# A retention layer with a soft mixture of experts: the keys by tokens of step 18 made on TensorE instead of loaded

## Chip, cores, metric

One core of a Trainium2 chip. The metric is the device time of one execution in microseconds; the table below gives the median of three.

## What is computed

Two layers in a row, all in float32. The first is a decaying linear attention (retention) over B = 4 sequences, H = 8 heads, S = 768 tokens, D = 64; the second a mixture of 8 experts with 4 slots each, in which every slot reads a weighted mean of all 3,072 tokens.

```python
for t in range(S):                                   # retention
    state = gamma[None, :, None, None] * state + np.einsum('bhd,bhe->bhde', k[:, :, t], v[:, :, t])
    y[:, :, t] = scale * np.einsum('bhd,bhde->bhe', q[:, :, t], state)
x = y as (B * S, H * D)
logits = x @ phi                                     # soft mixture of experts
d = softmax of logits over the tokens;  slot_input = d.T @ x
slot_out[e] = np.maximum(slot_input[e] @ w1[e], 0.0) @ w2[e]
out = (softmax of logits over the slots) @ slot_out
```

## The kernel before

**Steps and pairs.** The retention is done in chunks of 128 tokens. A step is one chunk of one sequence; there are 24 of them, numbered chunk by chunk (step i is sequence i mod 4, chunk i // 4), and worked on in twelve pairs (`P`, steps 2P and 2P + 1). Per step: scores of keys against queries (`score_mm`, L227), a causal mask on VectorE (L235), the part of the output that comes from the state (`carry_mm`, L251), the part from within the chunk (`attend_mm`, L260), the state's update from keys and values (`state_mm`, L288), the output turned to tokens-by-features (`natural_mm`, L304, copied by ScalarE at L311), and logits and dispatch sums (L328, L384).

**Two layouts of the keys.** The scores need the keys by features (`kT`, features on the partitions), the state needs them by tokens (`kn`, tokens on the partitions). For most steps both come from memory: the input tile holds `kT`, `qT`, `v` and `kn`, 512 columns each, one load of 128 x 2048 floats (L201, 1,024 KB). Steps in the list `TURNED` (L46) load only the first three (L199, 768 KB), and `turn_k` (L203) makes `kn`: four transposes of 128 x 128 on TensorE (L206) into a PSUM bank and one copy by ScalarE (L207) into the empty quarter of the input tile. The last four steps need no `kn`, since no state follows them. The host lays the two kinds of steps out in two arrays (`x3`, `x4`, L712).

**Order.** The order on every engine is written out by hand (`manual_schedule`, L94): what the program says first, the engine does first. In the loop over pairs (L451 to L528) pair P issues the loads of steps 2P + 6 and 2P + 7 on SyncE, between weight loads (`PACE`, L45); six input tiles go round, so a load waits until the step that used the tile is done. GpSimd multiplies the new queries and values by decays (L212, L217). `turn_k` of the even step 2P + 2 stands between the state's update and `natural_mm` of pair P (L501), and uses the bank "A0", which the scores of step 2P + 2 take next.

**Behind the retention.** From about 107 us TensorE multiplies the slots by the first expert weights (L589), then by the second (L669), and combines (L650); VectorE and ScalarE copy the results (L655), and SyncE writes them out in eight transfers of 768 KB (L656). All transfers of data, in and out, are issued by SyncE and go through one queue (queue 1) over 16 DMA engines. Queues 8 and 14 carry the engines' instructions.

```python
501  if 2 * P + 2 in TURNED:
502      turn_k(2 * P + 2, "A0")
503  natural_mm(P)
504  natural_copy(P)
```

Of the kernel before, what the change touches and what calls it, by code (L numbers as in the profile page):

```python
# [42 lines left out]
NIN = 6  # L43
NRING = 9
PACE = (1, 1, 1, 2, 1, 2, 1, 2, 2, 0, 2, 2)  # L45
TURNED = (0, 1, 2, 3, 4, 8, 12, 14)  # L46
SIW = 48
LEAN = [i for i in range(1, NSTEP) if i in TURNED or i >= NSTEP - B]
FULL = [i for i in range(1, NSTEP) if i not in LEAN]
# [32 lines left out]
def retention_soft_moe_kernel(  # L82
# [120 lines left out]
    def turn_k(i, name):  # L203
        kp = bank(name)
        for g in range(NPAIR):
            nc.tensor.transpose(kp[:, g * 128:(g + 1) * 128], st[i]["kT"][:, g, :], ident)  # L206
        nc.scalar.copy(st[i]["kn"], kp.rearrange("p (h d) -> p h d", d=D))  # L207
# [83 lines left out]
    def state_add(P):  # L291
        for k in range(2):
            d = sst[(2 * P + k) % B]
            if P < B // 2:
                nc.scalar.copy(d, pr[P]["S"][:, k])
            else:
                nc.vector.tensor_tensor(d, d, pr[P]["S"][:, k], ALU.add)  # L297
# [153 lines left out]
    for P in range(NPP):  # L451
# [46 lines left out]
        if P < NPP - B // 2:  # L498
            state_mm(P)
            state_add(P)  # L500
        if 2 * P + 2 in TURNED:  # L501
            turn_k(2 * P + 2, "A0")
# [235 lines left out]
```

## Time and profile before

| | |
|---|---|
| median of 3 executions | 158.36 us (158.28 to 158.56) |
| the profiled execution, its own time | 158.41 us |
| its span, first to last instruction | 156.6 us |
| mean granted clock of TensorE | 0.984 |
| busy: TensorE / VectorE / ScalarE / GpSimd | 92% / 50% / 27% / 38% |
| DMA: moved, mean rate | 62.48 MB, 399 GB/s |
| loads of 1,024 KB / of 768 KB for steps | 12 / 11 |

The span is what the trace covers; the execution's own time has 1.8 us around it. Busy shares are means over stages that differ: up to about 103 us the retention, then the experts, and behind 149 us nothing but writes. A DMA share of 1.00 is all 16 engines busy (a share a little over that is rounding of the records). "Landing" is the moment at which a transfer's semaphore says that all of it has arrived.

### The profile page before, as it was taken

How to read it: one execution, taken by the hardware profiler on the slowest of the kernel's cores; microseconds unless marked ns; L12 is line 12 of the kernel's file. 1: busy time of each engine (PE TensorE's matmuls, PEld its weight loads, DVE VectorE, ACT ScalarE, POOL GpSimd, SP SyncE). 2: the span in 40 equal slices, each digit the busy share in tenths (PEclk: the TensorE clock that was granted, in tenths of full speed). 3: DMA queues.
4: the chain of work that ended last, by engine and by line, in shares of the span. 5: the costliest groups of instructions: out<-in, count | busy, mean ns of one | idle time of the engine just before them, and what ended most of it. 6: DMA issues, size and time to landing. Idle time of an engine off the chain costs nothing.

```text
span 156.6 us, 5484 instructions
## 1 busy us (share of the span) xinstructions
PE 144.6 (92%) x2412; PEld 107.4 (69%) x2412; DVE 77.8 (50%) x187; ACT 42.2 (27%) x100; POOL 58.8 (38%) x66
## 2 busy tenths in 40 slices
PE   7999999999999999999999979999999999999500
PEld 2688989897988789979996857864232555557200
DVE  0379337682865483768574847566010104535500
ACT  3215422333232316220613042344100001424300
POOL 1351986784936294654938283010000000000000
PEclk9999999999999999999999999999999999999985
DMA  4999999999999999999999999999999999999891
GB/s 159 421 424 421 416 419 416 416 414 419 406 423 408 423 419 410 427 398 431 404 419 412 415 411 416 400 408 421 411 428 416 423 416 416 414 415 417 348 402 78
DMA packets 9816, 62.48 MB, mean 399 GB/s; under 512 B 1088, under 2 KB 1088, under 8 KB 4544
## 3 DMA queue, kind: packets, MB, share of 16 engines
q1 hardware_dynamic: 9792, 62.13, 96.6%
q8 instruction: 19, 0.31, 0.8%
q14 instruction: 5, 0.04, 0.1%
HBM read 55.84 MB, written 6.29 MB: 397 GB/s over the span
## 4 chain that ended last, share of the span: by engine, by line
PE 92%; DVE 2%; issue 1%; DVEq 0%
PE A L227 16%; PE Y L260 15%; PE A L669 9%; PE A L304 7%; PE Y L251 6%; PE S L288 6%; PE Y L589 4%; PE A L589 4%; PE sm L328 4%; PE sm L424 3%; PE S L384 3%; PE A L206 2%; PE sm L650 2%; PE S L650 1%; PE Y L650 1%; PE Y L638 1%
## 5 line engine op out<-in xcount | busy, mean ns | idle before, releaser
L235 DVE TENSOR_TENSOR r<-A,mi 128x512 f32<-128x512 f32 (+1 forms) x50 | 30.1, 662 | 22.1 <-PE A L227 22.1
L212 POOL TENSOR_TENSOR b<-b,qtab 128x512 f32<-128x512 f32 x20 | 25.7, 1287 | 23.5 <-DMA b<-in_x_dram 18.3
L227 PE MATMUL A<-b 64*128 64x128 f32 x384 | 25.4, 280 | 0.0
L227 PEld LDWEIGHTS A<-b 64*128 64x128 f32 x384 | 22.7, 188 | 3.1 <-issue 2.0
L217 POOL TENSOR_TENSOR b<-b,kt 128x512 f32<-128x512 f32 x23 | 23.6, 1046 | 2.4 <-DMA b<-in_x_dram 2.4
L260 PE MATMUL Y<-r,b 128*64 128x128 f32 x352 | 22.5, 276 | 0.5 <-issue 0.5
L260 PEld LDWEIGHTS Y<-r,b 128*64 128x64 f32 x352 | 19.2, 137 | 2.9 <-issue 2.6
L669 PE MATMUL A<-b,r 128*32 128x128 f32 (+1 forms) x336 | 15.9, 300 | 0.0
L311 ACT COPY r<-A 128x512 f32<-128x512 f32 x23 | 12.4, 592 | 8.6 <-PE A L304 8.6
L669 PEld LDWEIGHTS A<-b,r 128*32 128x32 f32 x336 | 10.3, 109 | 6.4 <-issue 4.4
L304 PE MATMUL A<-mi,r 128*128 128x128 f32 x96 | 13.3, 278 | 0.3 <-ACT r L279 0.3
L288 PE MATMUL S<-b 128*64 128x64 f32 x304 | 11.1, 222 | 0.6 <-issue 0.6
L304 PEld LDWEIGHTS A<-mi,r 128*128 128x128 f32 x96 | 10.4, 141 | 1.7 <-ACT r L279 0.5
L288 PEld LDWEIGHTS S<-b 128*64 128x64 f32 x304 | 10.4, 138 | 0.5 <-issue 0.5
L251 PE MATMUL Y<-b,sst 64*64 64x128 f32 x304 | 10.6, 276 | 0.0
L416 POOL TENSOR_TENSOR cn<-cn,cz 128x128 f32<-128x128 f32 x6 | 2.4, 401 | 19.6 <-DVE cz L415 7.2
L280 DVE COPY r<-Y 128x512 f32<-128x512 f32 x9 | 6.2, 690 | 5.9 <-PE Y L260 5.1
L251 PEld LDWEIGHTS Y<-b,sst 64*64 64x64 f32 x304 | 8.2, 132 | 1.2
L328 PEld LDWEIGHTS sm<-r,kt 128*32 128x32 f32 x192 | 6.2, 110 | 3.3 <-issue 3.3
L408 ACT ACTIVATE cn<-cn 128x128 f32<-128x128 f32 x6 | 1.9, 310 | 21.2 <-DVE cn L407 21.2
L328 PE MATMUL sm<-r,kt 128*32 128x128 f32 x192 | 7.4, 273 | 0.0
L297 DVE TENSOR_TENSOR sst<-sst,S 128x256 f32<-128x256 f32 x16 | 6.0, 418 | 2.7 <-PE S L288 2.5
(140 smaller groups left out, 182.9 us busy)
## 6 DMA issues: line engine op xcount, KB each, us to landing
b<-in_w_dram SPq DMA_DIRECT2D x29, 1024.0 KB, 15.1
b<-in_x_dram SPq DMA_DIRECT2D x12, 1024.0 KB, 12.5
b<-in_x_dram SPq DMA_DIRECT2D x11, 768.0 KB, 10.7
out_dram<-b SPq DMA_DIRECT2D x8, 768.0 KB, 8.7
r<-in_w_dram SPq DMA_DIRECT2D x5, 512.0 KB, 11.0
b<-in_first_dram SPq DMA_DIRECT2D x1, 512.0 KB, 3.5
r<-in_first_dram SPq DMA_DIRECT2D x1, 512.0 KB, 4.3
sst<-in_w_dram SPq DMA_DIRECT2D x1, 512.0 KB, 11.7
```

Of the source, the lines that this page charges most:

```text
L212: nc.gpsimd.tensor_tensor(q, q, qtab, ALU.mult)
L217: nc.gpsimd.tensor_tensor(v, v, vsc[:, i // B, a:b].unsqueeze(2).broadcast_to([128, b - a, D]), ALU.mult)
L227: nc.tensor.matmul(s["sc"][r][:, g, :], s["kT"][half(r), g, :], s["qT"][half(r), g, :], start=True, stop=True, skip_group_check=True)
L235: nc.vector.tensor_tensor(s["A"][:, r, g:g + n], s["sc"][r][:, g:g + n], mask.unsqueeze(1).broadcast_to([128, n, C]), ALU.mult)
L251: nc.tensor.matmul(p["y"][k][b][half(half_of(r, g)), gl, :], sst[(2 * P + k) % B][half(r), g, :], s["qT"][half(r), g, :], start=(gl == 0 a ...
L260: nc.tensor.matmul(pr[P]["y"][k][g // 2][half(half_of(r, g)), g % 2, :], s["v"][:, 2 * g + r, :], s["A"][:, r, g, :], start=(P < B // 2 an ...
L288: nc.tensor.matmul(S_[half(r), k, g, :], s["kn"][:, 2 * g + r, :], s["v"][:, 2 * g + r, :], start=True, stop=True, skip_group_check=True)
L304: nc.tensor.transpose(X[k][:, g * 128:(g + 1) * 128], pr[P]["yT"][:, k, g, :], ident)
L311: (nc.scalar.copy if engines[k] == "scalar" else nc.vector.tensor_copy)(xn, pr[P]["X"][k])
L328: nc.tensor.matmul(q["ltp"][32 * j:32 * j + 32, :], phis[:, p, :], st[GRP * g + j]["yT"][:, p, :], start=(p == 0), stop=(p == NPAIR - 1), ...
L589: nc.tensor.matmul(hp[hf][32 * j:32 * j + 32, :], si0[:, a:a + NSLOT], w1t[hf, g, k][:, j * 512:(j + 1) * 512], start=(g == 0 and k == 0), ...
L669: nc.tensor.matmul(op[32 * j:32 * j + 32, :w], hT[fc // 4][:, fc % 4, 4 * g + j, :], w2t[4 * g + j, cb, fc], start=(n == 0), stop=(n == le ...
```

## The change

Step 18 joins the list. Its load is one of 768 KB from the first array, where it takes a row of its own, and pair 8 gets a `turn_k`.

```diff
-TURNED = (0, 1, 2, 3, 4, 8, 12, 14)
+TURNED = (0, 1, 2, 3, 4, 8, 12, 14, 18)
 LEAN = [i for i in range(1, NSTEP) if i in TURNED or i >= NSTEP - B]
 FULL = [i for i in range(1, NSTEP) if i not in LEAN]
```

On TensorE, in pair 8 (steps 16 and 17): the state's update (L288), the outputs' transposes (L304), and the first transpose of the probabilities (L364); A_... are PSUM tiles of the four "A" banks, S and sm those banks.

```order
 L260 MATMUL Y_1200<-r,b 64x128 x4
 L288 MATMUL S<-b 64x64 x16
-L304 MATMUL A_1255<-mi,r 128x128 x4
-L304 MATMUL A_1260<-mi,r 128x128 x4
+L206 MATMUL A_1255<-mi,b 128x128 x4
+L304 MATMUL A_1261<-mi,r 128x128 x4
+L304 MATMUL A_1266<-mi,r 128x128 x4
 L364 MATMUL sm<-mi,pT 128x128
```

Four transposes of the keys come in ahead of the outputs' transposes; everything behind keeps its order.

On ScalarE, the same pair: the copy of half of the outputs out of PSUM (L279), and the copies of the turned outputs (L311).

```order
 L279 COPY r<-Y_1199 128x2x256
-L311 COPY r<-A_1255 128x512
-L311 COPY r<-A_1260 128x512
+L207 COPY b<-A_1255 128x512
+L311 COPY r<-A_1261 128x512
+L311 COPY r<-A_1266 128x512
 L369 COPY pl<-sm 128x128
```

One copy comes in ahead of the two.

On SyncE, the loads of pair 6 (steps 18 and 19, between weight loads), and what each issue waits for (the load before on its semaphore, and the engines that used the tile).

```order
 L163 DMA b<-in_w_dram 128x2048 [waits DMAHW3_49]
-L201 DMA b<-in_x_dram 128x2048 [waits PE_49,DMAHW4_49,Activation_49,Pool_49]
+L199 DMA b<-in_x_dram 128x1536 [waits PE_49,DMAHW4_49,Activation_49,Pool_49]
 L201 DMA b<-in_x_dram 128x2048 [waits DMAHW5_49,PE_49,Pool_49]
 L163 DMA b<-in_w_dram 128x2048 [waits DMAHW6_49]
```

The load of step 18 keeps its place and its waits, and is a quarter shorter. Later in the same queue, the weight load that takes over step 18's tile waits for ScalarE too.

## Rows read from the trace of the kernel before

**Rows 1.** The page: busy us of TensorE (share, instructions) with the other engines; the DMA share in tenths and the rate in 40 slices of the span.

```profile
PE 144.6 (92%) x2412; PEld 107.4 (69%) x2412; DVE 77.8 (50%) x187; ACT 42.2 (27%) x100; POOL 58.8 (38%) x66
...
DMA  4999999999999999999999999999999999999891
GB/s 159 421 424 421 416 419 416 416 414 419 406 423 408 423 419 410 427 398 431 404 419 412 415 411 416 400 408 421 411 428 416 423 416 416 414 415 417 348 402 78
```

**Rows 2.** The chain that ended last, by engine (page); and from the table of waits: who waited for what, us in total, times, longest.

```profile
PE 92%; DVE 2%; issue 1%; DVEq 0%
...
POOL b L212 <- DMA b<-in_x_dram: 18.3, 14, 2.7
...
PEld Y L589 <- issue: 3.8, 13, 0.3
...
PEld Y L589 <- DMA b<-in_w_dram: 0.6, 2, 0.3
```

**Rows 3.** The tail by stretches: from:to and length in us; busy us of PE, PEld, DVE, ACT, POOL (instructions); granted clock, DMA share, GB/s.

```profile
138.00:146.50 8.50, 7.70 (x168) 5.33 (x167) 3.79 (x10) 2.22 (x6) 0.00 (x0) 1.00 1.02 418
146.50:149.00 2.50, 1.30 (x16) 0.45 (x12) 1.82 (x4) 1.63 (x4) 0.00 (x0) 1.00 0.69 279
149.50:152.50 3.00, 0.00 (x0) 0.00 (x0) 0.00 (x0) 0.00 (x0) 0.00 (x0) 0.82 1.02 422
152.50:153.50 1.00, 0.00 (x0) 0.00 (x0) 0.00 (x0) 0.00 (x0) 0.00 (x0) 0.50 0.61 252
153.50:155.00 1.50, 0.00 (x0) 0.00 (x0) 0.00 (x0) 0.00 (x0) 0.00 (x0) 0.50 0.19 78
```

**Rows 4.** The last four writes of the output, two by two: the issues (first and last start in us), and the us from issue to landing (least, median, most: the first and the second of each two).

```profile
L656 SPq DMA_DIRECT2D out_dram<-b x2: 332/332/332, 142.2 to 143.8; - x2
...
DMA to landing us min/median/max: 7.9/8.0/8.0
...
L656 SPq DMA_DIRECT2D out_dram<-b x2: 332/332/333, 148.3 to 149.2; - x2
...
DMA to landing us min/median/max: 5.4/5.9/6.3
```

**Rows 5.** Transfers of instructions: both queues over the whole span (count, MB, share of 16 engines' time), then queue 8 from the start to 67.0, to 71.6 and to 135.7 us; then loads in issue order, each with its time to landing: the weights issued at 50.8, step 18's input, which is next in the queue, and two neighbours among the weights issued at 113.4 and 114.4.

```profile
q8 instruction: 19, 0.31, 0.8%
q14 instruction: 5, 0.04, 0.1%
...
q8 instruction: 8, 0.13, 0.8%
...
q8 instruction: 9, 0.15, 0.8%
...
q8 instruction: 17, 0.28, 0.8%
...
L163 SPq DMA_DIRECT2D b<-in_w_dram x1: 422/422/422, 50.8 to 50.8; - x1
...
DMA to landing us min/median/max: 16.8/16.8/16.8
...
L201 SPq DMA_DIRECT2D b<-in_x_dram x1: 328/328/328, 59.6 to 59.6; - x1
...
DMA to landing us min/median/max: 12.1/12.1/12.1
...
L166 SPq DMA_DIRECT2D b<-in_w_dram x2: 327/328/328, 113.4 to 114.4; - x2
...
DMA to landing us min/median/max: 18.4/19.9/21.4
```

**Rows 6.** The pace of loads: the first four of 768 KB (steps 1 to 4), and four neighbours of 1,024 KB (two inputs, then two weight tiles); first and last issue, and us from issue to landing, of which the least is the first load's and the most the last one's.

```profile
L199 SPq DMA_DIRECT2D b<-in_x_dram x4: 424/436/442, 1.7 to 3.1; - x4
...
DMA to landing us min/median/max: 5.8/7.9/10.0
...
L201 SPq DMA_DIRECT2D b<-in_x_dram x2: 328/344/359, 26.4 to 26.9; - x2
L163 SPq DMA_DIRECT2D b<-in_w_dram x2: 434/990/1547, 27.3 to 27.8; - x2
...
DMA to landing us min/median/max: 10.0/13.1/16.2
```

**Rows 7.** The chain in order of time (start, us, what) around the transposes of pair 6, which has a turned step, and of pair 8, which has none, and at the state's update of pair 9.

```profile
59.88 0.59 PE A L206 x4
60.46 0.87 PE A L304 x8
...
61.44 0.64 PE A L227 x7
...
76.08 1.02 PE A L304 x8
...
77.22 1.99 PE A L227 x32
...
82.13 0.81 PE S L288 x27
```

**Rows 8.** ScalarE in order of time (start, us, what; in brackets the idle time before) in pair 6 and in pair 8.

```profile
60.50 0.59 ACT L207 COPY b<-A 128x512 f32<-128x512 f32 x1 [1.11 <-PE A L206]
60.98 1.08 ACT L311 COPY r<-A 128x512 f32<-128x512 f32 x2
...
76.71 1.07 ACT L311 COPY r<-A 128x512 f32<-128x512 f32 x2 [0.77 <-PE A L304]
```

## The prediction

> **What bounds the kernel now.** I read four views. First the page's overall rows: TensorE is busy 92% of the span, and the DMA engines show a 9 in 37 of 40 slices, at about 415 GB/s [rows 1]. Both look full, so shares alone don't say which one the end hangs on. Second, what TensorE waits for: the chain that ended last is 92% PE, and the DMA waits of the engines end in the preparations on GpSimd (18.3 us of waiting before L212), which run ahead; TensorE's own wait for expert weights is 0.6 us in two pieces of 0.3, and 0.3 is also what its weight loads idle there when they wait for nothing [rows 2]. So TensorE runs from work to work, and a shorter load gives it nothing. A reading that stops here says: TensorE is the bound, four more transposes make the kernel longer.
>
> Third, the tail by stretches [rows 3]. TensorE has finished before 149, but the span goes on to 156.6. The DMA share is 1.02 up to 146.5, falls to 0.69 between 146.5 and 149, is full again from 149.5 to 152.5, drops to 0.61 and then stands at 0.19 from 153.5 to 155. 0.19 of 16 engines is three engines. So thirteen run dry while the last two writes are not yet issued, take them up when they are, and finish at about 153; three are still working for two more microseconds. Were all sixteen equal, the end would follow the issue of the last writes, and with it TensorE.
>
> Fourth, the last four writes from issue to landing [rows 4]. Issues are irregular: 142.2, 143.8, 148.3, 149.2. Landings are 142.2 + 7.9 = 150.1, 143.8 + 8.0 = 151.8, 148.3 + 5.4 = 153.7 and 149.2 + 6.3 = 155.5: 1.8 us apart each time, although 4.5 us lie between the second issue and the third. A transfer has landed when its slowest engine is done. The slowest engines therefore never ran dry: they deliver one write after another at their own pace, and their end is the sum of all that was ever queued on them, not the issue of the last write. The bound is the three late engines.
>
> Why three, and will they stay late? The page counts 19 instruction transfers of 16 KB on queue 8 [rows 5], 0.8% of 16 engines' time, or about 1.05 us each (0.008 x 16 x 156.6 / 19). Each sits on one engine. While the queue is full, two loads of 1,024 KB land 2.5 us apart [rows 6]. Twice in the middle of the kernel they don't [rows 5]: from 50.8 + 16.8 = 67.6 to 59.6 + 12.1 = 71.7, and from 113.4 + 18.4 = 131.8 to 114.4 + 21.4 = 135.8, 4.0 apart each. The slowest engine lost 1.5 us there. Queue 8 stands at eight transfers by 67.0 and at nine by 71.6; by 135.7 it stands at seventeen [rows 5]. The ninth and the seventeenth cost the slowest engine something, those between did not: the fetches go round eight engines, and 19 of them give three engines a third one. Three engines, as the share of 0.19 says.
>
> The Trainium skill (Runtime: NRT & Kernel Launch, Instruction fetch mechanics) says that crossing a 16 KiB instruction block costs one bump of a DMA tail and is mostly hidden. By that the three late engines would have no cause and the sum would be the one of the first rival below; the 4.0 us between two landings speaks against it, for the engine that carries the fetch, if not for TensorE.
>
> **The change part by part.** It moves step 18 from the steps loaded with all four blocks to those loaded with three, and makes the fourth, keys by tokens, on TensorE and ScalarE in pair 8.
>
> 1. *Removed: 256 KB of load.* Four loads of 1,024 KB land between 26.4 + 10.0 = 36.4 and 27.8 + 16.2 = 44.0, so 2.5 us apart (7.6 / 3); four of 768 KB between 1.7 + 5.8 = 7.5 and 3.1 + 10.0 = 13.1, so 1.9 apart (5.6 / 3) [rows 6]. The difference is 0.62 us, and 262,144 bytes at 418 GB/s [rows 3] are 0.63. I take 0.63. It comes off each of the 16 engines alike, so off the late three too; all that stands behind step 18's load in the queue moves up by as much. On the path: **-0.63 us**, if nothing starves the late engines afterwards.
>
> The Trainium skill (DMA: Bandwidth & Descriptors, Rules for kernel authors) wants 1 MiB or more in a DMA for the full rate, which speaks against cutting one down to 768 KB. The rows have both sizes at one rate: 768 KB in 1.9 us, 1,024 KB in 2.5.
>
> 2. *Added on TensorE: four transposes* (L206), between the state matmuls and the transposes of the outputs. Pair 6 has the same order, with step 14. There the four take 0.59 us of the chain and the eight of L304 behind them 0.87; in pair 8, without them, L304 takes 1.02 [rows 7]. So +0.59 - 0.15 = +0.44 us on TensorE from 76.1 on, with 0.59 as the upper end. This lies beside the transfers: it is no part of the sum while the late engines have work. It makes the issue of the last writes 0.44 later.
>
> 3. *Added on ScalarE: one copy of 0.59 us* (L207), ahead of the two copies L311, which come 0.5 to 0.6 later. In pair 6 the copy runs at 60.50 and L311 until 62.06 [rows 8]; the score matmuls, which overwrite those PSUM banks, start at 61.44 with no gap in the chain [rows 7], the second half of them a microsecond later. In pair 8 ScalarE is free from 75.9 to 76.7 [rows 8]. Cover: the score matmuls of the first step (1 us) for the second bank pair. If the cover failed, TensorE would wait up to 0.6 us, and I would have 0.44 + 0.6 = 1.04 us on TensorE. The copy's reader, the state matmul of pair 9, comes at 82.1 [rows 7], 5 us later.
>
> 4. *Moved or new waits.* Step 18's input is needed by L206 at 76.1; before, it landed at 71.7 [rows 5]. No wait. The weight load that later reuses step 18's buffer now waits for the copy too, but also, as before, for the state matmul that reads what the copy wrote, which is later. The input loads and weights behind SyncE's waits for TensorE come up to 0.44 us later into a queue that, by the 8 us from issue to landing, is many transfers deep. Price nothing. GpSimd: nothing moves.
>
> **Does the reserve hold?** The late engines take 1.8 us per write, end at 155.0, so start on the seventh at about 151.3; the others start on it between 149 and 149.5 [rows 3]. That is some 2.0 us of reserve. The change eats 0.63 + 0.44 = 1.07, at the worst 0.63 + 1.04 = 1.67. Seen from the end: the thirteen end at 153.0 + 0.44 = 153.4 (worst 154.0), the three at 155.0 - 0.63 = 154.4. The three stay last.
>
> **Sum:** the profiled execution took 158.41 us with a span of 156.6; 158.41 - 0.63 = 157.78. It stands 0.05 above the median of the three runs (158.36), so the forecast is **157.73 us**, likeliest range 157.5 to 158.0.
>
> **Rivals.**
> - *TensorE sets the end* (slower). The late three might be late only because they are slow at these writes, not because they have a backlog; then the whole tail follows the issue of the last two, 0.44 later: 158.80, up to 159.4 if the copy's cover fails. For it: the 92% of the chain, and 0.69 in 146.5 to 149, when many engines do wait for that issue. Against: landings at an even 1.8 us over uneven issues. It decides once TensorE's delay passes 1.4 us, or the reserve is that much smaller than I read. Chance 0.10.
> - *One fetch more on a late engine* (slower). Eight more PE instructions move the block borders; a further 16 KB on a late engine costs 1.5: 158.36 - 0.63 + 1.5 = 159.2. But a 20th would fall on the next engine, which has two. Chance 0.02.
> - *Nothing to be seen.* Most of the 0.63 is given back: a smaller instruction transfer (queue 14, five of them, about 0.5 us each from 0.1% of 16 engines' time [rows 5]) falls on one of the late three, or the reserve ends inside the last write. 158.05 to 158.6, say 158.2. Chance 0.13.
> - *More than the load.* The rotation of the fetches shifts and only two engines' worth of delay is left: up to 1.5 off before the thirteen engines hold the end, about 156.9. Chance 0.03.
> - That the change does not do what it says I rule out: step 18's load is cut in the program's own order.
>
> **How the numbers follow.** Forecast 0.72, the larger gain 0.03: faster 0.75. Same 0.13, slower 0.12. A difference under 0.2% (0.32 us) can't be told here; the runs before spread over 0.28. Forecast and the near half of "nothing to be seen" make 0.8: 157.45 to 158.35.
>
> **What would show it.** Right: the last landing 0.6 earlier with even steps of 1.8; a share near 0.19 at the very end; the seventh write issued near 148.7, 0.4 later; TensorE's end 0.4 later; landing of step 18 about 0.6 earlier; the hole at 147 to 149 wider by about 1 us. Wrong: the tail's even landings broken, with the last two following the issue by a fixed time; a gap in TensorE before L227 in pair 8; a different count on queue 8.

## The result and the profile after

The change is not faster. In the first series it took 159.49 us (median of 10, 158.43 to 159.96) beside 158.53 for before (158.19 to 158.81): ratio 1.0052 [1.003, 1.0075]. Two more series of the same two kernels gave 1.0001 [0.9978, 1.0024] and 1.0033 [1.0006, 1.006]. So by its three series it costs between nothing and 0.5%, and its executions scatter more widely than those of before. The forecast was 157.73, in a range of 157.45 to 158.35, faster with a chance of 0.75: wrong by 1.8 us in the first series, and no series is faster. The profiled execution, at 159.96, is the slowest of its series; one of the change at 158.28 is shown with the experiments.

The page of the change, as [rows 1]: TensorE, the DMA share and the rate in 40 slices, the fetch queue.

```profile
PE 145.4 (92%) x2416; PEld 108.0 (68%) x2416; DVE 78.3 (50%) x187; ACT 42.8 (27%) x101; POOL 58.6 (37%) x66
...
DMA  5999999999999999999999979899999999999982
GB/s 179 414 427 418 416 408 428 411 414 423 409 411 419 427 402 425 414 406 427 410 416 412 419 277 350 319 394 431 408 419 425 423 406 427 414 414 411 407 359 117
...
q8 instruction: 19, 0.31, 0.8%
```

TensorE is busy 0.8 us more, the fetches are 19 as before. What is new is at slices 24 to 26 (from about 91 us): 277, 350 and 319 GB/s, where before had 411, 416 and 400. The queue has a hole there, some 60 us ahead of the end and 15 behind the edit.

The last four writes of the change, as [rows 4], and its tail, as [rows 3].

```profile
L656 SPq DMA_DIRECT2D out_dram<-b x2: 332/332/333, 144.4 to 146.1; - x2
DMA to landing us min/median/max: 7.4/7.4/7.4
L656 SPq DMA_DIRECT2D out_dram<-b x2: 332/332/333, 150.5 to 151.5; - x2
DMA to landing us min/median/max: 4.7/5.2/5.6
```

```profile
149.00:151.50 2.50, 1.07 (x16) 0.34 (x8) 1.95 (x4) 1.63 (x4) 0.00 (x0) 1.00 0.74 299
151.50:155.00 3.50, 0.00 (x0) 0.00 (x0) 0.00 (x0) 0.00 (x0) 0.00 (x0) 1.00 1.01 418
155.00:157.20 2.20, 0.00 (x0) 0.00 (x0) 0.00 (x0) 0.00 (x0) 0.00 (x0) 0.57 0.14 56
```

The last write lands at 151.5 + 5.6 = 157.1; before it was 155.5. It is issued 2.3 us later, not 0.44. The share is full to 155.0, 2.1 us ahead of the last landing; before it was full to 152.5, 3.0 us ahead [rows 3]. So the late engines are 1.6 us later, in spite of the shorter load, and the others have lost part of their lead on top.

The hole, first in the kernel before, then in the change: from:to, length, busy us of PE, PEld, DVE, ACT, POOL, granted clock, DMA share, GB/s.

```profile
88.00:92.00 4.00, 3.50 (x74) 3.07 (x70) 3.09 (x9) 0.78 (x4) 1.44 (x2) 1.00 1.00 409
92.00:94.00 2.00, 1.66 (x15) 1.01 (x12) 0.69 (x1) 0.94 (x3) 2.00 (x2) 1.00 1.04 414
94.00:96.00 2.00, 2.00 (x37) 1.88 (x39) 1.02 (x3) 0.75 (x3) 1.50 (x3) 1.00 1.02 414
98.00:104.00 6.00, 6.00 (x84) 4.80 (x79) 3.69 (x12) 2.28 (x7) 0.40 (x1) 1.00 1.02 402
```

```profile
88.00:92.00 4.00, 4.00 (x89) 3.29 (x81) 3.54 (x9) 0.00 (x0) 1.88 (x3) 1.00 1.03 419
92.00:94.00 2.00, 1.30 (x25) 1.28 (x26) 1.12 (x6) 0.64 (x3) 2.00 (x2) 1.00 0.58 234
94.00:96.00 2.00, 1.64 (x18) 1.16 (x14) 0.69 (x1) 0.84 (x2) 1.45 (x3) 1.00 0.80 242
98.00:104.00 6.00, 6.00 (x104) 4.43 (x102) 4.39 (x12) 1.29 (x4) 0.00 (x0) 1.00 0.94 348
```

In 92 to 96 the transfers run at 238 GB/s instead of 414, and from 98 to 104 still at 348 instead of 402, with a share of 0.94.

Why it runs dry there: SyncE's wait, and the three weight loads L163 that are issued between 82 and 96 with their times to landing (the third, the first, the second), first in before, then in the change.

```profile
SPq L163 <- PE Y L260: 7.4, 1, 7.4
...
L163 SPq DMA_DIRECT2D b<-in_w_dram x3: 328/328/328, 82.7 to 91.4; - x3
DMA to landing us min/median/max: 7.8/11.5/13.1
```

```profile
SPq L163 <- PE Y L260: 7.6, 1, 7.6
...
L163 SPq DMA_DIRECT2D b<-in_w_dram x3: 327/328/328, 84.3 to 93.7; - x3
DMA to landing us min/median/max: 5.7/9.9/11.0
```

The third of them takes over the tile of step 20 (the next, L166, that of step 21), and so waits until TensorE has read that tile in the attend of pair 10 (L260). SyncE stands at that wait for 7.4 us, and at its end little more than the first two of these loads is outstanding; in before they land at 82.7 + 11.5 = 94.2 and 83.7 + 13.1 = 96.8. Before goes on at 91.4, and the share stays full. In the change the release comes 2.3 us later, and the share is 0.58 from 92 to 94. The bytes ahead of the place are 0.63 us fewer, but these two loads land at 94.2 and 96.7, as before: in this execution the slowest engine had already lost some 0.5 us by then.

### The profile page after: what moved, and what is told of

Its sections match the earlier page's. It is cut to its first block, busy times and chain, and to the rows that moved or that the text cites. A ratio compares the mean times of both kernels' runs of the same rounds, so it can differ in the third digit from the quotient of the medians.

```text
span 158.2 us, 5496 instructions
## 1 busy us (share of the span) xinstructions
PE 145.4 (92%) x2416; PEld 108.0 (68%) x2416; DVE 78.3 (50%) x187; ACT 42.8 (27%) x101; POOL 58.6 (37%) x66
## 3 DMA queue, kind: packets, MB, share of 16 engines
q1 hardware_dynamic: 9792, 61.87, 95.9%
## 4 chain that ended last, share of the span: by engine, by line
PE 83%; DMA 5%; DVE 4%; issue 2%; SPq 1%; ACT 1%; DVEq 0%; ACTq 0%
PE A L227 13%; PE Y L260 12%; PE A L669 9%; PE A L304 7%; PE S L288 6%; PE Y L251 6%; DMA b<-in_x_dram 5%; PE Y L589 4%; PE A L589 4%; PE sm L328 4%; PE S L384 3%; PE A L206 2%; DVE r L235 2%; PE sm L650 1%; PE S L650 1%
## 5 line engine op out<-in xcount | busy, mean ns | idle before, releaser
L212 POOL TENSOR_TENSOR b<-b,qtab 128x512 f32<-128x512 f32 x20 | 25.6, 1284 | 20.3 <-DMA b<-in_x_dram 10.7
L227 PE MATMUL A<-b 64*128 64x128 f32 x384 | 25.6, 282 | 0.1
L227 PEld LDWEIGHTS A<-b 64*128 64x128 f32 x384 | 22.9, 190 | 3.2 <-issue 1.8
L260 PE MATMUL Y<-r,b 128*64 128x128 f32 x352 | 22.5, 277 | 0.7 <-issue 0.7
L260 PEld LDWEIGHTS Y<-r,b 128*64 128x64 f32 x352 | 19.1, 137 | 3.2 <-issue 2.9
L311 ACT COPY r<-A 128x512 f32<-128x512 f32 x23 | 12.5, 594 | 7.8 <-PE A L304 7.8
L304 PE MATMUL A<-mi,r 128*128 128x128 f32 x96 | 13.3, 278 | 0.8 <-ACT r L279 0.7
L288 PE MATMUL S<-b 128*64 128x64 f32 x304 | 11.1, 222 | 1.3 <-issue 1.3
L304 PEld LDWEIGHTS A<-mi,r 128*128 128x128 f32 x96 | 10.5, 141 | 2.1 <-ACT r L279 1.1
L288 PEld LDWEIGHTS S<-b 128*64 128x64 f32 x304 | 10.4, 138 | 0.9 <-issue 0.9
```

The source lines that it names most:

```text
L212: nc.gpsimd.tensor_tensor(q, q, qtab, ALU.mult)
L227: nc.tensor.matmul(s["sc"][r][:, g, :], s["kT"][half(r), g, :], s["qT"][half(r), g, :], start=True, stop=True, skip_group_check=True)
L260: nc.tensor.matmul(pr[P]["y"][k][g // 2][half(half_of(r, g)), g % 2, :], s["v"][:, 2 * g + r, :], s["A"][:, r, g, :], start=(P < B // 2 an ...
L288: nc.tensor.matmul(S_[half(r), k, g, :], s["kn"][:, 2 * g + r, :], s["v"][:, 2 * g + r, :], start=True, stop=True, skip_group_check=True)
L304: nc.tensor.transpose(X[k][:, g * 128:(g + 1) * 128], pr[P]["yT"][:, k, g, :], ident)
L311: (nc.scalar.copy if engines[k] == "scalar" else nc.vector.tensor_copy)(xn, pr[P]["X"][k])
```

## The experiments

In every kernel three readings are compared: the rate in 92 to 96, the landing of the last write, and the time. The expectations call the theories by letters. Two decide in the end: A, TensorE's later issue of the last writes sets the end; and D, which took shape from the traces of the first runs, the queue of transfers runs dry at pair 10.

**The halves of the change.** Load only (the keys of step 18 read from step 19's):

```
-        if 2 * P + 2 in TURNED:
+        if 2 * P + 2 == 18:
+            st[18]["kn"] = st[19]["kn"]
+        elif 2 * P + 2 in TURNED:
```

> The short load alone: step 18 is loaded without its keys by tokens, nothing is transposed for it, and its state update reads step 19's keys by tokens instead (so that part is not computed). Theory A (the end follows TensorE once the queue of transfers has spent its reserve, and the turn makes TensorE late): TensorE ends where it did before, within 0.3 us, and the whole is the same to 0.6 us faster (157.9 to 158.5). Theory B (landings that move make GpSimd meet VectorE, and instruction transfers meet TensorE, at worse moments; the load does the harm): slower by 0.3 to 1 us, with TensorE's end 0.5 us or more later although it does no more work. Theory C (the prediction's: three late engines own the end): 0.6 us faster, 157.9.

Measured: 158.47, ratio 0.9998 [0.9979, 1.0016]. The shorter load alone, without the turn, gains nothing: its 0.63 is lost somewhere in the transfers. 303 GB/s in the stretch 92 to 96. That is in A's range; B wanted a loss and C, the prediction, 157.9: both miss.

Turn only (in before, a full load and the turn besides):

```
-        if 2 * P + 2 in TURNED:
+        if 2 * P + 2 in TURNED + (18,):
```

> The turn alone: step 18 is loaded in full as before, and its keys by tokens are made by transposes on top of what was loaded. Theory A: TensorE ends 0.4 to 1.5 us later, the last two writes with it, and the whole is 0.3 to 1.2 us slower. Theory B: same to 0.4 slower, since the landings have not moved. Theory C: same within 0.2 us, the late engines own the end and hide TensorE's 0.44.

Measured: 159.01, 1.0023 [1.0005, 1.004]. The turn is not hidden: 0.44 us on TensorE cost about 0.4 in the end, 70 us later. C, which had it hidden, fails here too.

The change and the kernel before once more, unedited:

> The change once more, for a second profile and for its spread. Theories A and B: 0.5 to 1 us slower than before, with executions from 158.4 to 160. Theory A: DMA share clearly under 1 between 91 and 96 us again, and the last write landing 5.6 us after its issue (6.3 before). Theory B: the extra stalls of TensorE stand at other places than in the first profile. Theory C would need 0.6 us faster.

> The kernel before once more, for a second profile. All theories: span 156.4 to 157, TensorE's last matmul near 147.8, DMA share 1.0 between 86 and 100 us. If TensorE's end moves by 1 us or more between two profiles of this same kernel, part of what the first profile of the change shows is its own spread.

The change again: 158.5 (158.19 to 159.8), 1.0001; its profiled execution took 158.28. The loss of 0.5 to 1 us that A and B expected did not show in this series; the share under 1 did (0.84). Before again: one execution, 158.39. The stretch 92 to 96 of the change's, then of before's second profile:

```profile
92.00:96.00 4.00, 3.63 (x48) 2.99 (x48) 0.97 (x3) 2.39 (x7) 2.74 (x4) 1.00 0.84 301
```

```profile
92.00:96.00 4.00, 3.65 (x49) 3.01 (x47) 1.15 (x5) 2.36 (x7) 3.60 (x4) 1.00 1.00 367
...
L656 SPq DMA_DIRECT2D out_dram<-b x2: 332/332/332, 149.1 to 150.0; - x2
DMA to landing us min/median/max: 4.7/5.2/5.6
```

The hole is in the quicker execution of the change too, only smaller. And TensorE of before issues the last write at 150.0 here, at 149.2 in [rows 4], with the same landing, 155.6 and 155.5: its issue doesn't set the end, and it moves by 0.8 us from one execution to the next.

**Whose end is it?** Three units of the last block's expert matmuls left out, in the change and in before:

```
+        if cb == 0:
+            units = units[:-3]
```

> The change, with three of the sixteen groups of products of the second expert weights left out in the first block of 256 columns (12 products, about 1.3 us of TensorE at 0.44 us a group; that part is not computed; all loads stay). Theory A (TensorE's end holds the change back): 0.4 to 0.8 us faster than before, 157.7 to 158.1, since TensorE is early again and the late DMA engines with the shorter load set the end. Theory D (the gain is lost in the hole in the transfers at 92 to 96 us, before these products): same as before, 158.4 to 158.6, with the writes landing 1.83 us apart.

> The kernel before with the same three groups of products left out. Both theories: the late DMA engines set the end of the kernel before, so 1.3 us less of TensorE gives 0 to 0.25 us (158.3 to 158.55), and the last write lands over 6.5 us after its issue. If it comes out 0.6 us or more faster, the kernel before already ended with TensorE, and the prediction's first reading is wrong from the start.

Measured: 159.25, 1.0046 [1.0027, 1.0064], and 158.61, 0.9995 [0.9982, 1.0007]. The last writes of before without those units:

```profile
L656 SPq DMA_DIRECT2D out_dram<-b x2: 332/332/333, 147.3 to 148.2; - x2
DMA to landing us min/median/max: 6.4/6.9/7.3
```

Issued 1.0 us earlier than in [rows 4], landed at 155.5 as there. So in before the late engines own the end, as predicted, and in the change an earlier TensorE at the end doesn't give the time back either. Theory A falls. D's figure, the same as before, is missed as well: the run is 0.5% slower. The hole (209 GB/s in 92 to 96) stays in the change.

A third series of the change, and one with its last two writes in halves of 384 KB, sent as soon as half of the columns are copied (core of the edit):

```
+                for js in ((0, 2), (2, 4)):
+                    for j in range(*js):
+                        (nc.scalar.copy if j % 2 else nc.vector.tensor_copy)(ot[:, :, j, :], cps[j])
+                    if tail:
+                        nc.sync.dma_start(dst[:, js[0]:js[1]], ob[:, js[0] * 3 * C:js[1] * 3 * C].rearrange("p (j x) -> p j x", j=2))
```

> The change for a third series, since two series gave 0.5% slower and no difference. Theory A: 0 to 0.8 us slower, and in the profile the last landing is either 5.0 us after the last issue (TensorE sets the end) or later by what a late engine still holds; TensorE's last issue 150.5 or later.

> The change with each of the two writes of the last 128 columns issued in two halves of 384 KB (two sequences each; the columns of a row are ordered by sequence first to keep long runs), so that the first half leaves after two copies out of PSUM and not after four. Theory A: the end follows the issues, so about 0.3 to 0.6 us faster than the change. Theory D: same as the change, since the late engines have to move the same bytes.

Measured: 158.98 (158.19 to 160.46), 1.0033, and 159.38, 1.0043 [1.0025, 1.0061]. The split, which A expected to help, did not. It is a weak sign against a loss at the tail: in both profiles with split writes (this one and the filled one below) the load of step 5 lands at 18.4 to 18.5, in all others at 16.8 to 17.2, so these executions were late long before. The rates in 92 to 96 were 193 and 203 GB/s.

**Filling the hole.** The weight loads into the tiles of steps 20 and 21 are cut into pieces, each issued once its part of the tile has been read: 512 columns behind the scores, 512 behind the state's part (carry), 1,024 behind the attend. The two loads of the last pair, into the tiles of steps 22 and 23, stay whole and move behind that pair's attend (core of the edit):

```
+        if P == NPP - 2:
+            early = [weight_at(st[i]["tile"]) for i in (NSTEP - 4, NSTEP - 3)]
+            for w in early:
+                load_piece(w, 0, 512)
...
+            for w in early:
+                load_piece(w, 512, 1024)
...
+            for w in early:
+                load_piece(w, 1024, 2048)
```

> The change, and the two weight loads that in pair 10 wait until the tiles of steps 20 and 21 are wholly free are cut into three pieces each (a quarter when the scores have read the keys, a quarter when the state part has read the queries, a half when the values are free too), so that two transfers of 256 KB enter the queue 3 to 4 us earlier, before it runs dry. Theory D (the queue runs dry at 92 to 95 us, and this costs more than the shorter load gives): DMA share near 1.0 between 92 and 96, 0.3 to 0.7 us faster than the kernel before (157.8 to 158.25), and 0.6 us or more faster than the change. Theory A (TensorE's end): as the change, 158.5 to 159.4.

> The kernel before with the same cut of the two weight loads. Theory D: it has hardly run dry there, so same, or up to 0.2 us faster (158.3 to 158.6), with fewer slow executions. If it is as fast as the change with the cut, the shorter load is worth nothing even with a full queue.

Measured: the change with it 158.06 (157.6 to 159.04), 0.9969 [0.9947, 0.999]; before with it 158.34 (158.26 to 158.45), 0.9978 [0.9964, 0.9992]. The change filled, its rate in 92 to 96, its six pieces and its last writes:

```profile
92.00:96.00 4.00, 3.40 (x40) 2.76 (x42) 1.36 (x5) 1.97 (x6) 2.77 (x4) 1.00 1.00 384
...
L180 SPq DMA_DIRECT2D b<-in_w_dram x6: 327/328/589, 89.2 to 94.1; - x6
...
L681 SPq DMA_DIRECT2D out_dram<-b x2: 332/332/332, 150.1 to 151.1; - x2
DMA to landing us min/median/max: 3.3/3.8/4.2
```

With the hole filled the change is faster than both kernels as they stood, by 0.5 us against before. But before gains 0.2% from the cut alone, and the two filled kernels can't be told apart: their intervals overlap (medians 158.06 and 158.34). What the cut does to before shows in its scatter: 12 executions within 0.2 us, where the 35 of before beside them run from 158.22 to 159.39. So before, too, loses time at this place in many of its executions. The filled change still scatters over 1.4 us. Its last write lands 4.2 us behind the issue, the least of all whole writes; whether the issue is what is left is tested below.

**A delay ahead of the hole and one behind it.** About 1 us of extra TensorE work in before, once ahead of pair 8, once in the expert phase at about 112 us:

```
+        if P == 8:
+            warm(2, "A0")
```

```
+                if (hf, g2, k) == (0, 1, 1):
+                    warm(2, "A0")
```

> The kernel before with two idle matmuls of zeros (1 us of TensorE) in pair 8, where the change puts its transposes; nothing else. Theory D: the tiles of pairs 9 and 10 come free 1 us later, the queue runs dry at 92 to 95, and the whole is 0.4 to 1.2 us slower (158.9 to 159.7). Theory A: slower by 0 to 0.5, by what 1 us exceeds the reserve at the end, and the same as with the delay at 112 us.

> The kernel before with the same two idle matmuls (1 us of TensorE) at about 112 us, among the products of the first expert weights, when the queue of transfers is deep again. Theory D: 0 to 0.3 us slower (the late engines own the end, reserve 0.6 to 1.3 us). Theory A: as the early delay.

Measured: early 159.27, 1.0033 [1.0018, 1.0049]; late 158.44, 0.9992 [0.9977, 1.0006]. The same work costs 0.5 us (by the ratio; 0.7 by the medians) ahead of the hole and nothing behind it. The two stretches 92 to 96, early, then late:

```profile
92.00:96.00 4.00, 3.25 (x38) 2.61 (x39) 1.48 (x5) 1.82 (x6) 3.46 (x4) 1.00 0.87 311
```

```profile
92.00:96.00 4.00, 3.65 (x49) 3.01 (x48) 1.15 (x4) 2.36 (x7) 3.62 (x4) 1.00 1.00 377
```

**What the load is worth with a full queue.** The fill with the shorter load alone, the filled change without the three units, and the filled change with split last writes (edits as above, combined):

> The short load alone (step 18's state update reads step 19's keys by tokens, so that part is not computed) with the two weight loads of pair 10 cut into pieces as before. If the queue is kept full, the load gives back its time as far as TensorE's end allows: 157.7 to 158.0, 0.4 to 0.6 us under the kernel before with the same cut (158.34). If the shorter load is worth nothing by itself: 158.3 to 158.4.

> The change with the cut weight loads, and three of the sixteen groups of products of the first block of the second expert weights left out (1.3 us of TensorE; not computed). If TensorE's end is what is left: 157.5 to 157.8, 0.55 to 0.8 us under the kernel before with the cut, and all executions within 0.3 us, since the late engines set the end; the writes then land 1.83 us apart with a spread between engines. If not: as the change with the cut, 158.06, with the same scatter.

> The change with the cut weight loads, and the last two writes issued in two halves each. In the profile of the change with the cut all engines end together, so the end follows the issues: a first half that leaves after two copies and not four should give 0.2 to 0.5 us (157.6 to 157.9). If short runs of 1,536 bytes or the second issue cost more: the same or slower.

Measured: 158.25, 0.9975 [0.9951, 0.9999], in two groups, six executions at 157.5 to 158.0 and six at 158.5 to 159.3; 157.95 (median of 7, 157.62 to 158.56), 0.9955 [0.9936, 0.9973]; 158.47, 0.9983 [0.9967, 1.0]. The first and the third miss the gains expected of them. The profiled execution of the first is one of the shorter group: 157.55 with 402 GB/s in the stretch; that of the second took 157.62 with 372. Against 158.34 for before filled these two are 0.8 and 0.7 quicker: the 0.63 of the load is there in single executions whose queue stays full. By the medians it is 0.1 and 0.4 only, since the longer executions give it back. The issue is not what is left: without the three units the last write is issued 1.0 us earlier than in the filled change (150.1, not 151.1) and lands 0.2 earlier, the intervals of the two overlap, and the executions spread over 0.9 us, not within 0.3.

The third run's profile is of a long execution, 159.31 us. Its stretches 92 to 96 and 96 to 98, then the load of step 5 there and in the filled change:

```profile
92.00:96.00 4.00, 2.99 (x47) 2.10 (x38) 2.59 (x8) 1.23 (x4) 3.42 (x4) 1.00 0.94 362
96.00:98.00 2.00, 1.95 (x25) 1.79 (x27) 0.16 (x1) 1.24 (x3) 0.23 (x1) 1.00 1.00 309
```

```profile
L213 SPq DMA_DIRECT2D b<-in_x_dram x1: 486/486/486, 3.7 to 3.7; - x1
DMA to landing us min/median/max: 14.7/14.7/14.7
```

```profile
L213 SPq DMA_DIRECT2D b<-in_x_dram x1: 445/445/445, 3.6 to 3.6; - x1
DMA to landing us min/median/max: 13.2/13.2/13.2
```

The transfers are nearly full in the stretch, and the end is late all the same: the slowest engine was 1.6 us behind at 18 us, long before step 18's load is issued. So the hole is not all that holds these executions up.

All profiled executions in the order of the rate in 92 to 96. Three landings are given: of the load ahead of the hole (the second L163 above), of the last load, and of the last write (last issue plus its time to landing, to 0.1). "Held" is the last one less 155.5, that of before, plus 0.63 where the load is short.

| kernel | third L163 issued | GB/s, 92 to 96 | load ahead lands | last load lands | last write lands | held, us |
|---|---|---|---|---|---|---|
| before | 91.4 | 414 | 96.8 | 140.8 | 155.5 | 0 |
| before, filled | in pieces | 407 | 96.9 | 141.0 | 155.8 | 0.3 |
| load only, filled | in pieces | 402 | 96.1 | 140.3 | 155.0 | 0.1 |
| before, less matmul | 91.8 | 395 | 96.7 | 140.8 | 155.5 | 0 |
| change, filled | in pieces | 384 | 96.0 | 140.4 | 155.3 | 0.4 |
| before, late delay | 92.1 | 377 | 96.8 | 140.9 | 155.6 | 0.1 |
| change, filled, less matmul | in pieces | 372 | 96.1 | 140.4 | 155.1 | 0.2 |
| before again | 92.2 | 367 | 96.8 | 140.9 | 155.6 | 0.1 |
| change, filled, split | in pieces | 362 | 97.5 | 141.8 | 156.6 | 1.7 |
| turn only | 92.9 | 344 | 96.8 | 141.5 | 156.3 | 0.8 |
| before, early delay | 93.3 | 311 | 96.7 | 142.0 | 156.7 | 1.2 |
| load only | 92.8 | 303 | 96.0 | 140.4 | 155.7 | 0.8 |
| change again | 92.8 | 301 | 95.9 | 140.8 | 155.5 | 0.6 |
| change | 93.7 | 238 | 96.7 | 141.1 | 157.1 | 2.2 |
| change, less matmul | 94.0 | 209 | 96.0 | 141.7 | 156.4 | 1.5 |
| change, split | 94.0 | 203 | 97.5 | 141.8 | 156.6 | 1.7 |
| change, third | 94.3 | 193 | 97.5 | 141.9 | 156.6 | 1.7 |

Down to 367 GB/s the end is held up by at most 0.4, from 362 down by 0.6 to 2.2. In the kernels without the cut, a release up to 92.2 is free, one at 92.8 is not.

Where it is lost differs. In before 44.0 us lie between the load ahead of the hole and the last load. In turn only, early delay, change again and change less matmul they are 44.7 to 45.7: there the slowest engine loses 0.7 to 1.7 us across the hole, having arrived on time (96.8, or 96.2 with the short load). In the change, change split, change third and change filled split it arrives 0.5 to 1.3 us late, and the hole adds 0.3 to 0.4. In the first profile of the change a further 1.3 us, in load only 0.6, come in the writes behind the last load. So the four largest rows of "held" are not the price of the hole alone.

How it came to be late in the third series: the last two input loads ahead of the hole, and the three L163.

```profile
L199 SPq DMA_DIRECT2D b<-in_x_dram x2: 327/332/336, 77.7 to 78.2; - x2
DMA to landing us min/median/max: 11.4/12.2/12.9
...
L163 SPq DMA_DIRECT2D b<-in_w_dram x3: 327/328/328, 85.2 to 94.3; - x3
DMA to landing us min/median/max: 5.7/9.8/11.2
```

The last input lands at 78.2 + 12.9 = 91.1, the next load at 85.2 + 9.8 = 95.0, 3.9 later and not 2.5, although it was issued long before. The two jumps in [rows 5] are as large, and the prediction put them down to transfers of instructions on the slowest engine. That the one here has the same cause fits, and isn't shown.

## Why the prediction was wrong

*Who owns the end of before:* right. Without three units of matmul the last write was issued 1.0 us earlier and landed at the same time. The Trainium skill (Perfetto Trace Analysis, What "DMA-bound" means) lists specific DMA engines among the things that can bind; [rows 3] and this run agree.

*Item 1, the load at -0.63 on the path:* right in size, and its condition, "if nothing starves the late engines afterwards", was the one that failed. Step 18 is issued at 60.2 and lands 10.7 later, at 70.9, 0.8 before [rows 5]. In the three filled profiles with the short load and whole writes the last load lands at 140.3 to 140.4, in before filled at 141.0: 0.6 to 0.7. Without the fill, load only is at 0.9998.

*Item 2, the transposes at +0.44 on TensorE:* right. The chain of the change in pair 8 (start, us, what), beside [rows 7]:

```profile
77.18 0.58 PE A L206 x4
77.76 0.87 PE A L304 x8
78.64 0.11 PE sm L364
78.75 1.31 PE A L227 x19
```

0.58 for the four, and 0.87 instead of 1.02 behind them: +0.43.

*Item 3, the copy hidden by the scores:* right, L227 follows without a gap.

*Item 4 is the step that failed:* "loads come up to 0.44 later into a queue that, by the 8 us from issue to landing, is many transfers deep. Price nothing." The 8 us are those of the last writes [rows 4]. At pair 10 hardly more than two loads are outstanding at the end of a wait of 7.4 us that stood in before's own table of SyncE's waits. The edit works on that place from both sides, since the content of the queue ends 0.63 earlier and the release comes 0.44 later. The price was 0.6 in the quicker execution of the change, which is the whole gain, lost across the hole. A delay of before alone, ahead of the place, cost 0.5 to 0.7; behind it, none. In the longer executions of the change and its variants 1.5 to 2.2 are held, and 0.3 to 1.7 of that is lost across the hole; the rest the prediction did not have either, and its cause is open.

*The reserve:* taken from one execution and from the tail alone, and from TensorE's delay as if it were the edit's 0.44 only. In the change's profile the issue is 2.3 us later, and much of that isn't the edit. TensorE comes to the edit's place at 77.18, where in before L304 starts at 76.08 [rows 7], 1.1 us later. It was held in pair 7 by VectorE's L407, and behind the edit's place by two gaps in which it waited for nothing that the profile shows. The chain of the change:

```profile
65.92 1.34 DVE cn L407
...
84.36 0.78 issue
...
92.03 0.70 issue
```

In before L407 takes 0.29, and the gaps are 0.33 and 0.50. But that profile is the exception: in the six others of kernels with the full load L407 takes 0.99 to 1.40. So the prediction read before's room from the luckiest of seven profiles, and the spread of 0.28 us that it took from three executions is 1.2 us over 35. It is scatter that both kernels have; before has a little room for it, the change none.

*The rivals:* the one on the slow side was TensorE at the tail; theory A of the runs, refuted. "Nothing to be seen", said as 158.2, has its range around the second series (158.5), by luck: the mechanism was a dry queue in the middle, which no rival named. "One fetch more" does not hold by its own sign, since queue 8 has 19 transfers as before; yet a jump of its size stands in the third series. *The signs:* even landings of the last writes were to tell late engines from a late issue. The change's land at 151.8, 153.5, 155.2 and 157.1, as evenly as before, so that sign tells nothing here; what told was the page's rate in slice 24.

*Open:* why the executions with the short load scatter by up to 1.8 us even with the fill (two groups in load only, filled), when before filled keeps within 0.2. The one profile of a long filled execution has the loss at 18 us, at the load of step 5; why it falls there isn't shown, and the longer group of load only has no trace. And the table is no formula: the change filled and split holds 1.7 us at 362 GB/s, load only 0.8 at 303.

## What to carry to other kernels

Before pricing a later issue at nothing, read the depth of its queue at that place: how many loads are outstanding while the issuing engine waits, and when the first engines finish them. A saving in transfers and a delay in the work that frees their buffers act on the same reserve, and the smallest reserve of the whole kernel counts, not that of its end. A load that waits for a whole tile can be cut so that each piece follows the last reader of its part; here that turned a change that cost up to 0.5% into one that is 0.3% faster than the kernel before, which itself gains 0.2% from the cut. And read a reserve from more than one execution: the one profile that the prediction had was the luckiest.

## What was not expected of the hardware

A dry queue costs after the engines are busy again: 348 GB/s in 98 to 104 in the change, 402 in before, with shares of 0.94 and 1.02. In the change's second profile the share is full and the rate low all the same:

```profile
98.00:104.00 6.00, 6.00 (x94) 4.48 (x89) 3.81 (x12) 1.64 (x4) 0.40 (x1) 1.00 1.01 370
```

What the engines do in those 6 us wasn't resolved.

VectorE's L407, 128 x 128, took 0.29 us in before and 1.32 in the change. GpSimd's L212 ran from 65.83, 0.09 ahead of it, to 67.10; in before both started at 65.28 and VectorE was done first. The rows of the change (start, us, engine, line):

```profile
65.83 1.27 POOL L212 TENSOR_TENSOR b<-b,qtab 128x512 f32<-128x512 f32 x1 [0.83 <-DMA b<-in_x_dram]
...
65.92 1.32 DVE L407 TENSOR_TENSOR cn<-lq,cm 128x128 f32<-128x128 f32 x1
```

L407 ends 0.14 behind L212, which points to a wait for it, though 0.14 is less than the 0.29 of before. The Trainium skill (SBUF — State Buffer, SBUF: two separate sides) calls the pair of ports that GpSimd shares with an instruction of VectorE that has two inputs in SBUF an exclusive lock: the one that starts first has it for the whole instruction. These rows agree in who waits; here a tenth of a microsecond decided who waits for 1 us.
